# Attention's state as an undecayed dense running sum, and the integer sum of the weights' conversion on VectorE

## The chip, the cores and the metric

The kernel runs on one core of a Trainium2 chip. The metric is the device time of one execution in microseconds (us). The engines are TensorE (PE; PEld is its weight load), VectorE (DVE), ScalarE (ACT), GpSimd (POOL) and SyncE (SP), which here only issues transfers (DMA). Each engine takes its instructions in a fixed order.

## The reference

A retention layer (attention without softmax, with a decay `gamma` of its own for each head) feeds a block with a rational activation, and that feeds a gated block behind an RMS norm. All is in float32; there are 4 sequences of 576 tokens, 8 heads of 64 and a width of 512, so 2304 tokens.

```python
scores = scale * np.matmul(q, k.transpose(0, 1, 3, 2))
Dmat = np.where(rel >= 0, gamma[:, None, None] ** rel[None, :, :], 0.0)   # rel = i - j
x = np.matmul(scores * Dmat, v)                      # [4, 8, 576, 64] -> [2304, 512]
h = x @ w_in                                         # 2048 wide
g = (a0 + a1*h + a2*h**2 + a3*h**3) / (1 + |b0|*|h| + |b1|*h**2 + 1e-6)
x = g @ w_out                                        # 512 wide
xn = x / sqrt(mean(x * x) + 1e-6) * rms_g
out = (silu(xn @ w_gate) * (xn @ w_val)) @ w_out2    # 1536 wide
```

## The kernel before

**Attention.** Each sequence is cut into 5 chunks of 128 tokens (the last has 64), which makes 20 steps. Step `i` works on all 8 heads, as 4 pairs: one head of a pair has its 64 dimensions on partitions 0 to 63, the other on 64 to 127 (`e` is 0 or 1). `att_scores` (L189) multiplies k and q of each pair on PE (L196) and lets DVE multiply the scores with the table `dmk` (L201); `att_out` (L225) adds to one PSUM bank the product of q with the state `S` (L232) and that of the masked scores with v (L238), scales it with `gq` into the one buffer `xe` (L245; the trace calls it `gx`), and sends this to DRAM (L249) or, for the first 384 tokens, splits it for the next block (L211, L212). `att_state` (L253) multiplies k and v (L261), and `att_add` adds this to the state (L275, L277).

The decay sits in four tables: `dmk` is the causal mask times a power of gamma for each key, k is scaled by `gk` on POOL for the state (`prep_k`, L187), the state is scaled by `gs` from one chunk to the next on ACT (`att_decay`, L221), and the output by `gq`. The state of a pair is a 128 x 128 matrix with zeros off the diagonal, in two buffers `SS`, since L232 multiplies both heads of a pair at once; so DVE writes it in two halves of 64 partitions. `dmk` is built at the start by eight products on POOL (L532).

**Weights.** They come as raw 64-bit words. `begin` (L134) turns a tile of 128 x 512 into float32 by hand: two activations on ACT (L141, L142), a shift and a merge on DVE (L143, L147), and the integer sum of high and low part on POOL (L150), after which the raw buffer (one of three) is loaded anew by SP (L129). `finish` (L154) rounds on ACT (L156) and takes the rest on DVE or, for each fourth tile, on POOL (L157). There are 32 tiles for the first block (`wa`) and 36 for the second (`wb`).

**The blocks.** The first block takes 6 blocks of 384 tokens through 16 steps each: `m1_up` (L308 to L310, 12 matmuls), the activation on ACT, DVE and POOL (`m1_el`, L329 to L369), and `m1_down` (L317 to L321, 12 matmuls) three steps later. The first token block runs beside the attention: `hook` places four pieces of a step of the attention between the matmuls, and `wa_step` the conversion of the weights. The norm between the blocks (`be_*`, L387 to L426) and the first weights of the second block lie beside the last steps. The second block is `m2_up` (L440 to L442) and `m2_down` (L457 to L459).

A scheduler with a model of the engines makes the final order of each engine from this program.

## Time and profile before

| what | us |
|---|---|
| median of 3 runs | 1006.39 |
| lowest and highest | 1004.44, 1006.87 |
| the profiled execution | 1000.21 |
| its span in the trace | 998.4 |
| mean granted clock of PE in it | 0.986 |

All rows are of that one execution; its span is shorter than its time by 1.8 us. Where PE is idle, or works at the lower level of its clock, time is lost; an engine that is idle elsewhere costs nothing by that. [...] Windows are counted from the span's start. A row's busy time is the time covered by instructions of that engine.

### The profile page before, as it was taken

How to read it: one execution, taken by the hardware profiler on the slowest of the kernel's cores; microseconds unless marked ns; L12 is line 12 of the kernel's file. 1: busy time of each engine (PE TensorE's matmuls, PEld its weight loads, DVE VectorE, ACT ScalarE, POOL GpSimd, SP SyncE). 2: the span in 40 equal slices, each digit the busy share in tenths (PEclk: the TensorE clock that was granted, in tenths of full speed). 3: DMA queues.
4: the chain of work that ended last, by engine and by line, in shares of the span. 5: the costliest groups of instructions: out<-in, count | busy, mean ns of one | idle time of the engine just before them, and what ended most of it. 6: DMA issues, size and time to landing. Idle time of an engine off the chain costs nothing.

```text
span 998.4 us, 14966 instructions
## 1 busy us (share of the span) xinstructions
PE 970.4 (97%) x5726; PEld 912.7 (91%) x5726; DVE 567.7 (57%) x993; ACT 548.1 (55%) x1076; POOL 390.7 (39%) x358
## 2 busy tenths in 40 slices
PE   8898998999999999999989999999999999999998
PEld 6798887899999999999989989999999999999997
DVE  5989997768667675776697685554212112112111
ACT  4777775776877877878868665554112112111111
POOL 4666674754654746646646423334001001000000
PEclk9899999999999999999999999999999999999999
DMA  9757676300100100001012343433101000000000
GB/s 315 267 174 219 227 239 209 119 5 32 33 1 32 33 33 19 14 32 32 23 56 93 110 136 127 127 125 101 48 1 34 31 1 30 19 1 9 24 1 32
DMA packets 37592, 78.91 MB, mean 79 GB/s; under 512 B 5904, under 2 KB 21392, under 8 KB 37520
## 3 DMA queue, kind: packets, MB, share of 16 engines
q1 hardware_dynamic: 36512, 77.61, 23.8%
q8 instruction: 45, 0.74, 0.3%
q10 hardware_dynamic: 1008, 0.34, 0.1%
q14 instruction: 27, 0.22, 0.1%
HBM read 64.57 MB, written 13.37 MB: 78 GB/s over the span
## 4 chain that ended last, share of the span: by engine, by line
PE 73%; DVE 11%; ACT 4%; issue 4%; DMA 4%; POOL 3%; DVEq 0%; ACTq 0%; SPq 0%; POOLq 0%
PE bank L440 9%; PE bank L442 9%; PE bank L441 9%; PE bank L308 5%; PE bank L458 5%; PE bank L459 5%; PE bank L457 5%; PE bank L310 5%; PE bank L309 5%; PE bank L317 5%; PE bank L318 5%; PE bank L321 4%; DVE w L157 1%; DMA raw<-in_w_out_dram 1%; DMA x_d<-gx 1%
## 5 line engine op out<-in xcount | busy, mean ns | idle before, releaser
L440 PE MATMUL bank<-x,w 128*128 128x384 f32 x528 | 177.2, 336 | 1.9 <-DVE sg L446 1.9
L442 PE MATMUL bank<-x,w 128*128 128x384 f32 x528 | 177.2, 336 | 0.0
L441 PE MATMUL bank<-x,w 128*128 128x384 f32 x528 | 177.0, 335 | 0.0
L446 DVE TENSOR_TENSOR sg<-sg,bank 128x384 f32<-128x384 f32 x72 | 39.8, 553 | 213.8 <-PE bank L442 213.7
L150 POOL TENSOR_TENSOR ft<-ft,raw 128x512 int32<-128x512 int32 x68 | 94.8, 1396 | 119.9 <-DVE ft L147 78.4
L308 PE MATMUL bank<-x,w 128*128 128x384 f32 x384 | 132.4, 346 | 5.1 <-DVE u L350 4.8
L348 POOL TENSOR_TENSOR q<-q,ah 128x384 f32<-128x384 f32 x96 | 101.4, 1057 | 85.2 <-ACT q L344 81.6
L309 PE MATMUL bank<-x,w 128*128 128x384 f32 x384 | 131.1, 341 | 1.3 <-DVE x L212 1.3
L310 PE MATMUL bank<-x,w 128*128 128x384 f32 x384 | 131.1, 341 | 0.0
L369 POOL TENSOR_TENSOR g<-u,g 128x384 fp32r<-128x384 f32 x96 | 100.8, 1051 | 69.5 <-issue 34.4
L317 PE MATMUL bank<-g,w 128*128 128x384 f32 x384 | 124.7, 341 | 3.2 <-ACT g L367 3.2
L318 PE MATMUL bank<-g,w 128*128 128x384 f32 x384 | 123.5, 338 | 0.6 <-POOL w L157 0.6
L445 ACT ACTIVATE sg<-bank 128x384 f32<-128x384 f32 x72 | 35.3, 490 | 152.6 <-PE bank L442 152.4
L212 POOL TENSOR_TENSOR x<-xr,x 128x384 fp32r<-128x384 f32 x44 | 46.5, 1069 | 158.0 <-ACT x L211 157.8
L440 PEld LDWEIGHTS bank<-x,w 128*128 128x128 f32 x528 | 99.1, 188 | 5.6 <-DVE sg L446 2.2
L441 PEld LDWEIGHTS bank<-x,w 128*128 128x128 f32 x528 | 99.1, 188 | 3.0 <-POOL x L212 0.3
L442 PEld LDWEIGHTS bank<-x,w 128*128 128x128 f32 x528 | 99.1, 188 | 0.1
L448 ACT ACTIVATE y<-sg 128x384 fp32r<-128x384 f32 x72 | 37.6, 523 | 100.7 <-DVE sg L446 99.9
L349 DVE TENSOR_TENSOR u<-u,bank 128x384 f32<-128x384 f32 x96 | 52.9, 551 | 60.3 <-ACT u L345 59.5
L321 PE MATMUL bank<-g,w 128*128 128x384 f32 x384 | 85.3, 336 | 0.0
L308 PEld LDWEIGHTS bank<-x,w 128*128 128x128 f32 x384 | 73.7, 192 | 8.3 <-DVE u L350 6.6
L317 PEld LDWEIGHTS bank<-g,w 128*128 128x128 f32 x384 | 71.4, 189 | 5.3 <-ACT g L367 4.0
(92 smaller groups left out, 2042.6 us busy)
## 6 DMA issues: line engine op xcount, KB each, us to landing
raw<-in_w_out_dram SPq DMA_DIRECT2D x28, 512.0 KB, 3.7
xb<-in_qkT_dram SPq DMA_DIRECT2D x19, 512.0 KB, 4.9
kv<-in_kv_dram SPq DMA_DIRECT2D x16, 512.0 KB, 5.3
raw<-in_w_in_dram SPq DMA_DIRECT2D x16, 512.0 KB, 4.1
raw<-in_w_gate_dram SPq DMA_DIRECT2D x12, 512.0 KB, 3.4
raw<-in_w_val_dram SPq DMA_DIRECT2D x12, 512.0 KB, 3.4
xn_d<-x SPq DMA_DIRECT2D x6, 768.0 KB, 3.8
xr<-xn_d SPq DMA_DIRECT2D x24, 192.0 KB, 2.5
```

Of the source, the lines that this page charges most:

```text
L150: pool.tensor_tensor(out=ft, in0=ft, in1=lo, op=ALU.add)
L308: pe.matmul(out=h, lhsT=w[:, 0, ks], rhs=x[:, 0, k], start=(k == 0), stop=False)
L309: pe.matmul(out=h, lhsT=w[:, 0, ks], rhs=x[:, 1, k], start=False, stop=False)
L310: pe.matmul(out=h, lhsT=w[:, 1, ks], rhs=x[:, 0, k], start=False, stop=(k == KD - 1))
L317: pe.matmul(out=acc[m], lhsT=w[:, 0, ms], rhs=g[:, 0], start=(j == 0), stop=False)
L318: pe.matmul(out=acc[m], lhsT=w[:, 1, ms], rhs=g[:, 0], start=False, stop=False)
L321: pe.matmul(out=acc[m], lhsT=w[:, 0, ms], rhs=g[:, 1], start=False, stop=(j == J1 - 1))
L348: pool.tensor_tensor(out=q, in0=q, in1=ah, op=ALU.mult)
L369: eng.tensor_tensor(out=g[:, 1], in0=p, in1=g[:, 0].bitcast(F32), op=ALU.subtract)
L440: pe.matmul(out=t, lhsT=w[:, 0, ks], rhs=x[:, 0, k], start=(k == 0), stop=False)
L441: pe.matmul(out=t, lhsT=w[:, 0, ks], rhs=x[:, 1, k], start=False, stop=False)
L442: pe.matmul(out=t, lhsT=w[:, 1, ks], rhs=x[:, 0, k], start=False, stop=(k == KD - 1))
```

## The change

The decay leaves the state, the scores and k. Each v is scaled by gamma to minus its position (counted from the middle of the sequence), the output by gamma to its position, and the scores only get the causal mask of zeros and ones. So the state is a plain running sum of k times v: `att_decay` and its 48 activations go, `S` is one buffer without the zeros, and DVE updates it in one instruction on 128 partitions. The product of q with the state becomes 8 matmuls on 64 x 64 quarters of the array instead of 4 on the whole. POOL scales v (`prep_v`) where it scaled k, also in the last chunk, and its eight products for the table fall away; `gq` has a table for each of the five chunks, four of them loaded by SP in the first steps. In the last chunk the keys of the second head lie on partitions 64 to 127, and k isn't loaded. `xe` has a buffer of its own; it is still one.

The integer sum of each weight tile moves from POOL to DVE, all 68 of them. [...]

```diff
-    gk = at_p.tile([128, NH, 1], F32, name="gk")
-    gs = at_p.tile([128, NP, 1], F32, name="gs")
-    gi = at_p.tile([128, NH, 1], F32, name="gi")
+    gv = at_p.tile([128, NC, NH, 1], F32, name="gv")
+    msk = at_p.tile([128, 1, CH], F32, name="msk")
...
-    dmk = borrow("dmk").rearrange("p (e n c) -> p e n c", e=2, n=NP)
-    gx = borrow("gx").rearrange("p (a n c) -> p a n c", a=2, n=NP)
-    gq, xe = gx[:, 0], gx[:, 1]
-    SS = [at_p.tile([128, NP, 2, HD], F32, name=f"S{i}") for i in range(2)]
+    gq = []
+    for i in range(2):
+        t = borrow(f"gq{i}").rearrange("p (a n c) -> p a n c", a=2, n=NP)
+        gq += [t[:, 0], t[:, 1]]
+    gq.append(at_p.tile([128, NP, SEQ - (NC - 1) * CH], F32, name="gq4"))
+    xe = at_p.tile([128, NP, CH], F32, name="xe")
+    S = at_p.tile([128, NP, HD], F32, name="S")
...
-            pool.tensor_tensor(out=ft, in0=ft, in1=lo, op=ALU.add)
+            dve.tensor_tensor(out=ft, in0=ft, in1=lo, op=ALU.add)
...
+    def keys(i, e):
+        n = size(steps[i][1])
+        return n, slice(0, n) if n == CH else slice(n * e, n * e + n)
...
     def load_kv(i, dq=sp):
         if i < len(steps):
-            n = size(steps[i][1])
-            dq.dma_start(out=kv_b[i % 3][0:n], in_=kv[steps[i]][0:n])
-
-    def prep_k(i, eng):
-        if i < len(steps) and steps[i][1] < NC - 1:
-            k = kv_b[i % 3][:, 0]
-            eng.tensor_tensor(out=k, in0=k, in1=gk.to_broadcast([128, NH, HD]), op=ALU.mult)
+            c = steps[i][1]
+            if c < NC - 1:
+                dq.dma_start(out=kv_b[i % 3], in_=kv[steps[i]])
+            else:
+                n = size(c)
+                for e in range(2):
+                    dq.dma_start(
+                        out=kv_b[i % 3][n * e:n * e + n, 1], in_=kv[steps[i]][0:n, 1]
+                    )
+
+    def prep_v(i, eng):
+        if i < len(steps):
+            v = kv_b[i % 3][:, 1]
+            eng.tensor_tensor(
+                out=v, in0=v, in1=gv[:, steps[i][1]].to_broadcast([128, NH, HD]), op=ALU.mult
+            )
+
+    def load_gq(c):
+        if c < NC:
+            n = size(c)
+            sp.dma_start(out=gq[c], in_=t_gq[c, :, :, 0:n])
...
-                out=sc[0:n, p, 0:n], lhsT=qk[r, 1, p, 0:n], rhs=qk[r, 0, p, 0:n],
+                out=sc[ks, p, 0:n], lhsT=qk[r, 1, p, 0:n], rhs=qk[r, 0, p, 0:n],
...
-            out=rets[i, e][0:n, :, 0:n], in0=sc[0:n, :, 0:n], in1=dmk[0:n, e, :, 0:n], op=ALU.mult
+            out=rets[i, e][ks, :, 0:n], in0=sc[ks, :, 0:n],
+            in1=msk[ks, :, ks].to_broadcast([n, NP, n]), op=ALU.mult,
...
-    def att_decay(i):
-        c = steps[i][1]
-        if 0 < c < NC - 1:
-            for p in range(NP):
-                act.activation(
-                    out=SS[(c + 1) % 2][:, p], in_=SS[c % 2][:, p], func=ACTF.Copy, scale=gs[:, p]
-                )
...
             for p in range(NP):
-                pe.matmul(
-                    out=o[:, p, 0:n], lhsT=SS[c % 2][:, p].rearrange("p a d -> p (a d)"),
-                    rhs=q[:, p, 0:n], start=(p == 0), stop=False, skip_group_check=True,
-                )
+                for e in range(2):
+                    r = slice(64 * e, 64 * e + 64)
+                    pe.matmul(
+                        out=o[r, p, 0:n], lhsT=S[r, p], rhs=q[r, p, 0:n],
+                        start=(p == 0), stop=False, skip_group_check=True,
+                    )
         for p in range(NP):
             for e in range(2):
                 pe.matmul(
-                    out=o[64 * e:64 * e + 64, p, 0:n], lhsT=v[0:n, 2 * p + e],
-                    rhs=rets[i, e][0:n, p, 0:n], start=(c == 0 and p == 0), stop=(p == NP - 1),
+                    out=o[64 * e:64 * e + 64, p, 0:n], lhsT=v[keys(i, e)[1], 2 * p + e],
+                    rhs=rets[i, e][keys(i, e)[1], p, 0:n], start=(c == 0 and p == 0), stop=(p == NP - 1),
                     skip_group_check=True,
                 )
         t0 = b * SEQ + c * CH
         xo = xe[:, :, 0:n]
-        dve.tensor_tensor(out=xo, in0=o[:, :, 0:n], in1=gq[:, :, 0:n], op=ALU.mult)
+        dve.tensor_tensor(out=xo, in0=o[:, :, 0:n], in1=gq[c][:, :, 0:n], op=ALU.mult)
...
         if not pend:
             return
         c, ds = pend.pop()
-        new = SS[(c + 1) % 2]
-        for e in range(2):
-            r = slice(64 * e, 64 * e + 64)
-            if c == 0:
-                dve.tensor_copy(out=new[r, :, e], in_=ds[r])
-            else:
-                dve.tensor_tensor(out=new[r, :, e], in0=new[r, :, e], in1=ds[r], op=ALU.add)
+        if c == 0:
+            dve.tensor_copy(out=S, in_=ds)
+        else:
+            dve.tensor_tensor(out=S, in0=S, in1=ds, op=ALU.add)
...
     def att_jobs(kind, first, end):
         for i in range(first, end):
             att_add()
-            att_decay(i)
             load_kv(i + 2)
+            load_gq(i + 1)
             att_scores(i + 1, 0, kind)
             yield
...
-            prep_k(i + 1, pool)
+            prep_v(i + 1, pool)
...
-    for i in range(2):
-        dve.memset(SS[i], 0.0)
+    dve.memset(xe, 0.0)
     dve.memset(ones, 1.0)
-    warm = SS[0].rearrange("p n a d -> p (n a d)")
+    warm = xe.rearrange("p n c -> p (n c)")
...
-    act.dma_start(out=gq, in_=t_gq)
+    act.dma_start(out=msk, in_=t_dm)
     for a in range(2):
         sp.dma_start(out=qk_b[0][:, a], in_=qkT[0, 0, :, a])
-    act.dma_start(out=dmk[:, 0, 0], in_=t_dm)
-    act.dma_start(out=gi, in_=t_gi)
-    dmk8 = dmk.rearrange("p e n c -> p (e n) c")
-    for h in range(NH - 1, -1, -1):
-        pool.tensor_tensor(
-            out=dmk8[:, h], in0=dmk8[:, 0], in1=gi[:, h].to_broadcast([128, CH]), op=ALU.mult
-        )
+    act.dma_start(out=gq[0], in_=t_gq[0])
     act.activation(out=qb, in_=ones[:, 0:2], func=ACTF.Abs)
     load_kv(0, sp)
-    act.dma_start(out=gk, in_=t_gk)
-    act.dma_start(out=gs, in_=t_gs)
+    act.dma_start(out=gv, in_=t_gv)
...
-    t_gq = (HD ** -0.5) * g_pair[:, :, None] ** pos
-    t_gk = (gam[None, :] ** (CH - pos)[:, None])[:, :, None]
-    t_gs = (g_pair ** CH)[:, :, None]
+    rel = (np.arange(NC * CH) - SEQ // 2).reshape(NC, CH)
+    t_gq = (HD ** -0.5) * g_pair[None, :, :, None] ** rel[:, None, None, :]
+    rel[-1, CH // 2:] = rel[-1, :CH // 2]
+    t_gv = gam ** (-1.0 * rel.T[:, :, None])
     t_dm = pos[None, :] >= pos[:, None]
-    t_gi = (gam[None, :] ** (-1.0 * pos[:, None])).reshape(CH, NP, 2).transpose(0, 2, 1)
...
```

The order moves with it. On DVE, in the first steps of the attention, where `ret` are masked scores, `S` the state, `ft` and `w` the weights in conversion, before:

```order
L201 TENSOR_TENSOR ret<-bank_103,dmk 128x512
L143 TENSOR_SCALAR ft<-ft 128x512
L245 TENSOR_TENSOR gx<-bank_105,gx 128x512
L147 SCALAR_TENSOR_TENSOR ft<-raw,ft 128x512
L201 TENSOR_TENSOR ret<-bank_102,dmk 128x512
L143 TENSOR_SCALAR ft<-ft 128x512
L212 TENSOR_TENSOR x<-gx,x 128x4x128
L147 SCALAR_TENSOR_TENSOR ft<-raw,ft 128x512
L201 TENSOR_TENSOR ret<-bank_103,dmk 128x512
L157 TENSOR_TENSOR w<-ft,w 128x512
L277 TENSOR_TENSOR S_115<-S_115,bank_104 64x4x64 x2
```

and now (L219 was L201, L258 was L245, L231 was L212, L287 was L277):

```order
L258 TENSOR_TENSOR xe<-bank_105,gq_112 128x512
L147 SCALAR_TENSOR_TENSOR ft<-raw,ft 128x512
L143 TENSOR_SCALAR ft<-ft 128x512
L219 TENSOR_TENSOR ret<-bank_102,msk 128x512
L150 ISA ft<-raw,ft 128x1024
L231 TENSOR_TENSOR x<-xe,x 128x4x128
L147 SCALAR_TENSOR_TENSOR ft<-raw,ft 128x512
L219 TENSOR_TENSOR ret<-bank_103,msk 128x512
L157 TENSOR_TENSOR w<-ft,w 128x512
L287 TENSOR_TENSOR S<-S,bank_104 128x256
L150 ISA ft<-raw,ft 128x1024
```

The sums stand in DVE's row two or three instructions behind the merge (L147), and a state's update is one instruction.

On SP at the end of the attention, where `x_d<-` stores a step's output and `xr<-x_d` loads the next token blocks, before:

```order
L249 DMA x_d<-gx 512x1x128
L182 DMA kv_111<-in_kv_dram 64x1024
L249 DMA x_d<-gx 512x1x128 x2
L479 DMA xr<-x_d 128x384 x2
L249 DMA x_d<-gx 512x1x64
L479 DMA xr<-x_d 128x384 x2
```

and now (L262 was L249, L489 was L479):

```order
L262 DMA x_d<-xe 512x1x128
L191 DMA kv_110<-in_kv_dram 64x512 x2
L262 DMA x_d<-xe 512x1x128
L489 DMA xr<-x_d 128x384 x2
L262 DMA x_d<-xe 512x1x128
L489 DMA xr<-x_d 128x384 x2
L262 DMA x_d<-xe 512x1x64
```

Two pairs of loads stand ahead of the last store now, where one stood before. On PE, between the last two steps' products with v, there are 23 matmuls of the first block before and 50 now.

On DVE beside the norm of the fifth token block, some 500 us into the trace (`ss` is the norm's sum, `x_4840<-` its product with the tokens, `q`, `u` and the banks belong to the activation of the last block), before:

```order
L329 SCALAR_TENSOR_TENSOR q<-q,bank_105 128x384
L415 TENSOR_TENSOR ss<-ss,y 128x384
L329 SCALAR_TENSOR_TENSOR q<-q,bank_104 128x384
L330 SCALAR_TENSOR_TENSOR bank_105<-q,bank_105 128x384
L416 SCALAR_TENSOR_TENSOR ss<-ss,y 128x384
L349 TENSOR_TENSOR u<-u,bank_103 128x384
L330 SCALAR_TENSOR_TENSOR bank_104<-q,bank_104 128x384
L332 SCALAR_TENSOR_TENSOR u<-u,cf,bank_105 128x384
L421 SCALAR_TENSOR_TENSOR x_4840<-x_4840,rg,ss 128x384 x4
L350 SCALAR_TENSOR_TENSOR u<-u,cf,bank_103 128x384
```

and now (each of these lines is ten further down):

```order
L339 SCALAR_TENSOR_TENSOR q<-q,bank_105 128x384
L150 ISA ft<-raw,ft 128x1024
L425 TENSOR_TENSOR ss<-ss,y 128x384
L339 SCALAR_TENSOR_TENSOR q<-q,bank_104 128x384
L340 SCALAR_TENSOR_TENSOR bank_105<-q,bank_105 128x384
L359 TENSOR_TENSOR u<-u,bank_103 128x384
L426 SCALAR_TENSOR_TENSOR ss<-ss,y 128x384
L340 SCALAR_TENSOR_TENSOR bank_104<-q,bank_104 128x384
L342 SCALAR_TENSOR_TENSOR u<-u,cf,bank_105 128x384
L360 SCALAR_TENSOR_TENSOR u<-u,cf,bank_103 128x384
L431 SCALAR_TENSOR_TENSOR x_4841<-x_4841,rg,ss 128x384 x4
```

The last reader of bank_103 (L350, now L360) has moved from behind the four products of the norm to ahead of them.

## Rows read from the trace of the kernel before

**Rows 1.** The page, part 1: busy us (share of the span) x instructions.

```profile
PE 970.4 (97%) x5726; PEld 912.7 (91%) x5726; DVE 567.7 (57%) x993; ACT 548.1 (55%) x1076; POOL 390.7 (39%) x358
```

**Rows 2.** Windows: us, busy us of each engine (x instructions), PE's clock, DMA share, GB/s.

```profile
11.00:32.00 21.00, 17.63 (x194) 14.83 (x192) 20.64 (x32) 13.53 (x30) 9.46 (x9) 1.00 0.93 317
11.00:169.00 158.00, 148.11 (x1236) 130.38 (x1234) 144.16 (x240) 112.54 (x227) 99.68 (x80) 0.95 0.73 238
169.00:205.00 36.00, 31.71 (x221) 29.98 (x222) 24.82 (x43) 26.14 (x56) 27.32 (x25) 0.91 0.30 92
205.00:495.00 290.00, 288.91 (x1653) 286.39 (x1653) 206.66 (x383) 226.88 (x456) 165.72 (x166) 1.00 0.08 24
495.00:520.00 25.00, 21.09 (x111) 20.50 (x110) 22.56 (x40) 19.13 (x38) 11.23 (x11) 0.93 0.15 53
```

**Rows 3.** Waits of DVE, 11 to 169 us (us, times, longest), and POOL's timeline.

```profile
DVE ret L201 <- POOL dmk L532: 9.1, 1, 9.1
DVE u L349 <- ACT u L345: 2.4, 4, 1.5
DVE q L329 <- ACT bank L361: 1.9, 3, 0.9
...
11.11 1.04 POOL L187 TENSOR_TENSOR kv<-kv,gk 128x512 f32<-128x512 f32 x1
```

**Rows 4.** Groups of DVE by line and form, 11 to 169 us: busy us, mean ns.

```profile
L147 DVE SCALAR_TENSOR_TENSOR ft<-raw,ft 128x512 int32<-128x512 int32 x29 | 25.6, 883 | 0.3
L157 DVE TENSOR_TENSOR w<-ft,w 128x512 fp32r<-128x512 f32 x21 | 21.7, 1038 | 0.1
L201 DVE TENSOR_TENSOR ret<-bank,dmk 128x512 f32<-128x512 f32 x31 | 21.2, 683 | 9.6 <-POOL dmk L532 9.1 <-PE bank L196 0.4
L143 DVE TENSOR_SCALAR ft<-ft 128x512 int32<-128x512 int32 x29 | 16.7, 574 | 0.0
...
L277 DVE TENSOR_TENSOR S<-S,bank 64x256 f32<-64x256 f32 x20 | 8.3, 415 | 0.1
...
L275 DVE COPY S<-bank 64x256 f32<-64x256 f32 x8 | 3.3, 418 | 1.4 <-PE bank L261 1.3
```

**Rows 5.** Lines L147, L157 and L143, 0 to 205 us: shortest/median/longest ns.

```profile
L147 DVE SCALAR_TENSOR_TENSOR ft<-raw,ft x32: 676/694/1662, 15.1 to 184.7; 128x512 int32<-128x512 int32 x32
...
L157 DVE TENSOR_TENSOR w<-ft,w x24: 678/983/1551, 20.1 to 187.8; 128x512 fp32r<-128x512 f32 x24
...
L143 DVE TENSOR_SCALAR ft<-ft x32: 405/420/1402, 14.2 to 183.2; 128x512 int32<-128x512 int32 x32
```

**Rows 6.** Groups of POOL, 11 to 169 us: busy us, mean ns | idle before.

```profile
L150 POOL TENSOR_TENSOR ft<-ft,raw 128x512 int32<-128x512 int32 x29 | 39.5, 1367 | 26.6 <-issue 8.8 <-DVE ft L147 6.3 <-ACT ft L141 3.5
```

**Rows 7.** Timeline of PE (start, us), and a piece of the chain.

```profile
13.02 1.09 PE L238 MATMUL bank<-ret,kv 128*64 128x128 f32 x16
16.97 1.16 PE L232 MATMUL bank<-xb,S 128*128 128x128 f32 x8
...
126.35 0.17 PE bank L309
```

**Rows 8.** Timeline of SP and DVE at the end of the attention.

```profile
162.46 0.53 SPq L249 DMA_DIRECT2D x_d<-gx  x1
...
169.05 0.69 DVE L245 TENSOR_TENSOR gx<-bank,gx 128x512 f32<-128x512 f32 x1 [2.34 <-DMA x_d<-gx]
```

**Rows 9.** Waits from 500 to 512 us, and DVE's timeline there.

```profile
PE bank L308 <- DVE u L350: 3.9, 1, 3.9
...
503.09 0.54 DVE L329 SCALAR_TENSOR_TENSOR q<-q,bank 128x384 f32<-128x384 f32 x1
503.55 1.20 DVE L415 TENSOR_TENSOR ss<-ss,y 128x384 f32<-128x384 f32 x1
...
507.93 2.93 DVE L421 SCALAR_TENSOR_TENSOR x<-x,rg,ss 128x384 f32<-128x384 f32 x4
510.78 0.60 DVE L350 SCALAR_TENSOR_TENSOR u<-u,cf,bank 128x384 f32<-128x384 f32 x1
```

More of the change, by code (lines that the diff above doesn't have):

```diff
@@ L52, in retention_moe_kernel @@
     t_gq: bass.AP,
-    t_gk: bass.AP,
-    t_gs: bass.AP,
+    t_gv: bass.AP,
     t_dm: bass.AP,
-    t_gi: bass.AP,
     out: bass.AP,
@@ L191, in att_scores @@
             return
-        n = size(steps[i][1])
+        n, ks = keys(i, e)
         qk, r = qk_b[i % 3], slice(64 * e, 64 * e + 64)
@@ L548, in retention_moe_kernel @@
     att_scores(0, 1, "h")
-    prep_k(0, pool)
+    prep_v(0, pool)
     for s, _ in enumerate(att_jobs("h", 0, P0)):
@@ L752 @@
         ("t_gq", t_gq.astype(np.float32)),
-        ("t_gk", t_gk.astype(np.float32)),
-        ("t_gs", t_gs.astype(np.float32)),
-        ("t_dm", t_dm.astype(np.float32)),
-        ("t_gi", t_gi.reshape(CH, NH, 1).astype(np.float32)),
+        ("t_gv", t_gv[..., None].astype(np.float32)),
+        ("t_dm", t_dm[:, None].astype(np.float32)),
     ]
```

## The prediction

> **What bounds the kernel now.** Read the busy shares first: TensorE (PE) is busy for 97% of the span [rows 1], so only the stretches where it isn't can give or take time. The windows view finds them [rows 2]: from 205 to 495 us PE is busy 288.91 of 290 us, and nothing that VectorE (DVE), ScalarE (ACT) or GpSimd (POOL) saves there reaches the end. PE idles in three places: 11 to 169 us (the attention beside the first token block), 169 to 205 (its end), and 495 to 520. In the first, DVE is busy 144.16 of 158 us, 91%, and PE 148.11, but at a mean clock of 0.95; PE's busy time there holds waits between pipelined matmuls, DVE's does not. I take DVE as the engine that sets the pace there, with ACT (112.5) and POOL (99.7) in second place. This matters because the change takes work from POOL and ACT and gives work to DVE.
>
> **The change part by part, 11 to 169 us.** This is DVE's account; 29 of the 68 weight tiles are converted in this stretch [rows 4].
> - Added: 29 integer sums on DVE. No row shows this instruction. Below, it can't be cheaper than L147, which goes through the same 512 words from two SBUF tensors: 0.676 us at the least [rows 5]. Above, its stream is 1024 half words; L201 takes 0.683 us for 512 elements and L329 0.54 for 384 [rows 4, 9], so 1024 one by one would take 0.683 + 4 x 0.143 = 1.25 us. I take the lower end, since the row that it is nearest to in words moved is L147's. Consecutive DVE instructions overlap a little: the L329 at 503.09 takes 0.54 and the next starts 0.46 later [rows 9]; less 0.08, one sum occupies 0.60: 29 x 0.60 = +17.4.
> [...]
> - Removed: the state was updated in two halves of 64 partitions, now in one instruction. A half takes 0.415 us [rows 4], the whole has as many elements in a lane and costs the same: 14 fewer x 0.35 occupied = -4.9.
> - Contention. DVE's instructions with two SBUF operands, and L143, are slower while POOL works: L147 0.883 us in the mean against 0.676 at the least, L157 1.038 against 0.678, L143 0.574 against 0.405 [rows 4, 5]; together 29 x 0.207 + 21 x 0.360 + 29 x 0.169 = 18.5 us, with POOL busy for 63% of the stretch [rows 2]. POOL loses 39.5 us of sums (L150) [rows 6] and gains three more products of 1.04 us [rows 3] (v of the last chunk is scaled too): 99.7 - 39.5 - 0.4 + 3.1 = 62.9, about 39%. The exposed work grows from 29 x (0.676 + 0.405) + 21 x 0.678 = 45.6 to 65.3 us. Scaled by both: 18.5 x 65.3 / 45.6 x 39 / 63 = 16.4, so -2.1.
> - Sum: DVE's work goes from 144.2 to 154.6 us, +10.4.
> - The start: DVE's first product waited 9.1 us for POOL's last mask product, which ended when POOL went on at 11.11 [rows 3] and is gone now (the mask now comes whole by DMA). The next gates are the first scores and the coefficients' DMA, which stands ahead of the product in the new order; I take -1.0 (0 to -1.2).
> How much of +10.4 reaches the end hangs on DVE's idle 14 us. If DVE fills 96% (it was 20.64 of 21 us in the first part, 98% [rows 2]; 91% over all), the stretch starting at 10.2 ends at 10.2 + 154.6 / 0.96 = 171.2 instead of 169: **+2.2**. At 91% it ends at 180 (+11), at 100% at 164.8 (-4.2).
>
> ACT loses its 48 small scalings of the state. DVE waits for ACT only 4.3 us in the stretch [rows 3], so I count nothing of it by itself; what it shortens is part of how well DVE fills. Four more loads of the output's decay (3 x 256 KB + 128 KB = 0.92 MB) go onto SP's queue ahead of the fourth chunk's q, k and v. DMA is 93% busy from 11 to 32 us [rows 2], so those land later by 0.92 MB at 317 GB/s = 2.9 us; the third chunk's work, which comes first, lies over that: nothing (0 to +2).
>
> On PE the product of q with the state goes from 4 full-array matmuls to 8 on diagonal quarters of the array. Before, 4 of them take 1.16 us (8 records); v's product, 8 matmuls of 64 columns, takes 1.09 for 16 records, so two halves of the array run together [rows 7]. If the quarters do so too, 1.16 becomes 1.09: 16 steps, -1 us of PE time, nothing at the end. If they don't, each step costs 2.2.
>
> [...]
>
> **169 to 205 us.** At the end of the attention each of its 20 steps waits for the single output buffer: the 17th step's output leaves at 162.46, DVE waits 2.34 us for that store and writes the 18th's at 169.05 [rows 8], 6.6 us a step. Under this the old order has 23 MoE matmuls between the last two steps' outputs, at 0.17 us [rows 7] 3.9 us; the new has 50, 8.5 us, and that covers the loop. It also puts the second token block's loads (xr) one step earlier on SP's queue. PE idles 4.3 us in this window, with a clock of 0.91 [rows 2]. I take the uncovered part, 6.6 - 3.9 = **-2.7** (0 to -5).
>
> **495 to 520 us.** PE waits 3.9 us for L350 [rows 9], which frees a bank. L350 stands behind the four L421 (2.93 us from 507.93) in DVE's queue, and ends at 511.38. In the new order it stands ahead of them. Counting on from the L329 at 503.09 in steps of what each occupies: 503.56, sum 0.60, L415 0.47 (it took 1.20 beside POOL's sum, which is gone), L329, L330, L349 3 x 0.47, L416 0.9, L330 0.47, L332 0.53, L350 0.60: 508.5. That is **-2.9**. [...]
>
> From 520 to 700 us the other 36 sums stand where PE, saturated or nearly so, hides them.
>
> **The sum.** +2.2 - 2.7 - 2.9 = -3.4 us. The profiled execution took 1000.21 us (span 998.4), 6.2 less than the median of 1006.39; I take the difference over to the median: 1003.0.
>
> **The rivals.**
> - A, slower: DVE doesn't fill better. It is idle because the work passes in turn through PE, ACT and DVE, so it stays at 91%, and the stretch ends at 180. For it: 2.4 + 1.9 us of DVE's idle time are waits for ACT in this very loop [rows 3]. Against: 98% in the first part. +11 - 2.7 - 2.9 = +5.4: 1012. Below a filling of about 94% (10.2 + 154.6 / 0.94 = 174.7, +5.7) it outweighs the two gains and the kernel is slower than before.
> - B, slower: the half words pass one by one. 29 x 0.57 x 1.2 for contention = 20 us more on DVE; at 96% that is +21 - 3.4: 1024.
> - C: the quarters don't run together: 12 full steps x 1.1 + 4 half ones x 0.55 = 15 us more on PE, of which its 9.9 idle us in the stretch [rows 2] and the 2.2 of its lengthening hide most: +3, or up to +8 where PE's idle pieces lie elsewhere than the steps; 1008. [...]
> - D, no change: the new order's gains at 169 to 205 and 507 aren't there, because engines reach those places at other times; +2.2 remains: 1008.6 with nothing of them, 1006 with half.
> - E, faster: the loop through POOL decided more than DVE's load. L150 waited and kept the raw buffer from its next load (8.8 us of idle time before it with no cause shown, [rows 6]); the sum now follows two or three instructions behind L147 on the same queue. DVE fills 100%: -4.2 - 5.6 = -9.8: 997.
>
> **How the numbers follow.** Chances: forecast 0.37, A 0.18, B 0.06, C 0.11, D 0.16, E 0.12. About 0.3% (3 us) is what a measurement of this kernel can tell from no change, and the forecast at -3.4 lies on that edge: of its 0.37, 0.22 is faster and 0.15 the same. With E 0.12, faster 0.34; same is 0.15 + D's 0.12 + C's 0.05 = 0.32; slower is A, B, the rest of C and D: 0.34. Range for 8 in 10: 996 (just under E) to 1014 (A and C, with 2 us for the start's loads); it leaves out B. The forecast's own range is 998 to 1007.
>
> **What the profile after would show.** DVE's sum (L150) at 0.6 to 0.7 us where POOL is idle, its mean near 0.8; 1.2 or more would be B. DVE's busy share to the 18th step's output 95 to 97% for the forecast, 91% for A, with that output near 171 us against 169. The state's product (16 records) in about 1.1 us; 2.2 would be C. L147 and L157 nearer to their least. No wait of PE for the u of L350's successor over 1.5 us near 507, and from 169 to 205 less PE idle than 4.3 us. I am wrong if DVE's work in the stretch grew by much less or more than 10 us, or if the new order puts a new stall of PE after 205 us, which I have not found.

## The result: faster by 1.0%, three times the forecast

The changed kernel takes 994.29 us in the median of 8 runs (988.04 to 999.02), the kernel before beside it 1006.63: ratio 0.990, 95% interval 0.987 to 0.993, 10 us less. Forecast were 1003.0, 3.4 less, with a range down to 996: 994.29 lies 1.7 below that end, and the ratio applied to the 1006.39 that the forecast started from gives 996.1, just on it. The sign holds; the size doesn't. Over the later runs of this study and all runs of the changed kernel, the kernel before has a median of 1003.4 (94 runs), the changed one of 994.0 (18): 9.4 us. I use these two below.

The runs of one kernel differ by up to 14 us (before) and 11 us (changed), so one profile of each would mislead. Two executions of each were profiled: before at 1000.21 and 1008.09 us, after at 997.74 and 987.93. To compare them I cut each at one instruction of TensorE that all share: the sum over partitions for the norm of the fifth block (L404, in the changed kernel L414). What lies ahead of it is the **head** (it holds the attention), what lies behind, to the end of the span, the **tail**. The timeline's rows (start, us of all, matmul records) of before, before again, after, after again:

```profile
498.39 0.81 PE L404 MATMUL bank<-ss,ones 128*128 128x384 f32 x2
...
505.01 0.81 PE L404 MATMUL bank<-ss,ones 128*128 128x384 f32 x2
...
498.49 0.81 PE L414 MATMUL bank<-ss,ones 128*128 128x384 f32 x2
...
488.73 0.81 PE L414 MATMUL bank<-ss,ones 128*128 128x384 f32 x2
```

With spans of 998.4, 1006.3, 995.8 and 986.0 the tails are 500.0 and 501.3 before, 497.3 and 497.3 after: the tail hardly varies and is 3.4 us shorter. The heads vary by 7 to 10 us between executions of one kernel. Medians less the tail and the 1.8 or 1.9 us outside the span put the head at 500.9 before and 494.8 after: 6.1 us of the gain lie there. The second profile of each kernel is called "again" below.

The page and the windows of after (997.74 us), answering to [rows 1, 2]; columns as there:

```profile
PE 971.1 (98%) x5854; PEld 909.9 (91%) x5854; DVE 588.3 (59%) x1044; ACT 530.5 (53%) x1026; POOL 296.8 (30%) x286
...
11.00:32.00 21.00, 18.48 (x170) 15.28 (x166) 16.95 (x28) 9.62 (x16) 3.73 (x3) 0.75 0.95 339
169.00:205.00 36.00, 35.60 (x297) 32.48 (x298) 24.70 (x44) 21.74 (x44) 19.81 (x20) 0.91 0.38 113
495.00:520.00 25.00, 22.75 (x127) 21.53 (x126) 22.25 (x41) 19.50 (x39) 10.10 (x10) 1.00 0.16 52
```

TensorE's idle time from 169 to 205 us went from 4.3 us to 0.4, and from 495 to 520 us it is busy 22.75 us at a clock of 1.00 (of full speed) instead of 21.09 at 0.93. The first window shows where the heads begin to scatter. Here it is again in the other execution of after and the other one of before:

```profile
11.00:32.00 21.00, 18.66 (x209) 15.60 (x208) 19.62 (x33) 10.51 (x18) 4.59 (x4) 1.00 1.00 365
...
11.00:32.00 21.00, 20.60 (x168) 17.90 (x164) 16.72 (x28) 11.75 (x27) 7.53 (x6) 0.67 0.72 248
```

Both kernels have executions in which the clock stays at 1.00 in this window and executions in which it falls for most of it (0.75 and 0.67 in the mean; in after it is at 0.50 from 22 to 38 us), with the same order of instructions. With the fall, TensorE does 170 records instead of 209 (before: 168 instead of 194).

VectorE's groups of after, 11 to 169 us, answering to [rows 4], and the sum's shortest, median and longest ns up to 205 us, answering to [rows 5]:

```profile
L147 DVE SCALAR_TENSOR_TENSOR ft<-raw,ft 128x512 int32<-128x512 int32 x29 | 24.7, 861 | 0.2
L150 DVE CUSTOM_DVE_ANT_0 ft<-raw,ft 128x1024 uint16<-128x1024 uint16 x29 | 24.3, 839 | 0.2
L157 DVE TENSOR_TENSOR w<-ft,w 128x512 fp32r<-128x512 f32 x21 | 16.2, 770 | 0.4 <-ACT w L156 0.3
L143 DVE TENSOR_SCALAR ft<-ft 128x512 int32<-128x512 int32 x29 | 15.4, 537 | 2.8 <-ACT ft L141 2.7
L287 DVE TENSOR_TENSOR S<-S,bank 128x256 f32<-128x256 f32 x9 | 3.7, 411 | 0.0
...
L150 DVE CUSTOM_DVE_ANT_0 ft<-raw,ft x32: 670/683/1659, 15.8 to 189.9; 128x1024 uint16<-128x1024 uint16 x32
```

The sum of a tile's 512 words is one instruction over 1024 half words (uint16), which takes 0.670 us at the least and 0.839 in the mean. The state's update is one instruction of 0.41 us instead of two.

### The profile page after: what moved, and what is told of

The parts are those of the page before. It is cut to its first block, busy times and chain, and to the rows that moved or that the text cites. A ratio compares the mean times of both kernels' runs of the same rounds, so it can differ in the third digit from the quotient of the medians.

```text
span 995.8 us, 15066 instructions
## 1 busy us (share of the span) xinstructions
PE 971.1 (98%) x5854; PEld 909.9 (91%) x5854; DVE 588.3 (59%) x1044; ACT 530.5 (53%) x1026; POOL 296.8 (30%) x286
## 5 line engine op out<-in xcount | busy, mean ns | idle before, releaser
L231 POOL TENSOR_TENSOR x<-xr,x 128x384 fp32r<-128x384 f32 x44 | 46.2, 1063 | 284.1 <-ACT x L230 284.1
L327 PE MATMUL bank<-g,w 128*128 128x384 f32 x384 | 128.0, 340 | 2.3 <-ACT g L377 2.2
L328 PE MATMUL bank<-g,w 128*128 128x384 f32 x384 | 126.5, 335 | 0.0
L450 PEld LDWEIGHTS bank<-x,w 128*128 128x128 f32 x528 | 99.1, 188 | 5.7 <-DVE sg L456 0.9
L451 PEld LDWEIGHTS bank<-x,w 128*128 128x128 f32 x528 | 99.1, 188 | 3.0 <-POOL x L231 0.3
L452 PEld LDWEIGHTS bank<-x,w 128*128 128x128 f32 x528 | 99.1, 188 | 0.4
L331 PE MATMUL bank<-g,w 128*128 128x384 f32 x384 | 86.6, 336 | 0.0
L318 PEld LDWEIGHTS bank<-x,w 128*128 128x128 f32 x384 | 73.7, 192 | 10.1 <-DVE u L342 5.0
L320 PEld LDWEIGHTS bank<-x,w 128*128 128x128 f32 x384 | 73.7, 192 | 0.5 <-issue 0.3
```

The lines of the kernel that those rows point to most:

```text
L318: pe.matmul(out=h, lhsT=w[:, 0, ks], rhs=x[:, 0, k], start=(k == 0), stop=False)
L320: pe.matmul(out=h, lhsT=w[:, 1, ks], rhs=x[:, 0, k], start=False, stop=(k == KD - 1))
L327: pe.matmul(out=acc[m], lhsT=w[:, 0, ms], rhs=g[:, 0], start=(j == 0), stop=False)
L328: pe.matmul(out=acc[m], lhsT=w[:, 1, ms], rhs=g[:, 0], start=False, stop=False)
L331: pe.matmul(out=acc[m], lhsT=w[:, 0, ms], rhs=g[:, 1], start=False, stop=(j == J1 - 1))
L450: pe.matmul(out=t, lhsT=w[:, 0, ks], rhs=x[:, 0, k], start=(k == 0), stop=False)
```

## The experiments

**The two parts apart.** Theory "order": the gain sits where the order of instructions changed. Rival "loop" (E of the prediction): it comes from taking GpSimd out of the conversion's chain. The sum alone is one line in the kernel before; the attention alone is the changed kernel with that line undone.

```diff
-            pool.tensor_tensor(out=ft, in0=ft, in1=lo, op=ALU.add)
+            dve.tensor_tensor(out=ft, in0=ft, in1=lo, op=ALU.add)
```

> The kernel before with one line changed: the integer sum on VectorE; the attention stays as it was. Theory order: the gain of the whole change sits in two places where the order of instructions changed, 169 to 205 us and 495 to 520 us, and neither is new here (27 rather than 50 records between the last two outputs, and L350 still stands behind the four norm products), while VectorE carries about 8 us more net work up to 169 us: 1008 to 1014 us, and the wait of 3.9 us for L350 near 507 us is still there. Rival loop (rival E of the prediction): taking GpSimd out of the conversion's chain is what gains, so the sum alone gives most of it: 997 to 1001 us.

> The changed kernel with the integer sum back on GpSimd: the change of the attention alone. Theory order: VectorE has about 5 us less work up to 169 us, the start is 2 us earlier, and 169 to 205 us has the new order (-2.8), while L360 still stands behind the norm products near 507 us: 999 to 1003 us. Rival loop: GpSimd keeps its sums and gets three more products, so only the start and the end of the attention gain: 1002 to 1006 us, and the sum alone (e1) has the rest.

The sum alone: 1015.03 us, ratio 1.011 (1.008 to 1.015), slower. The attention alone: 996.54 us, ratio 0.992 (0.989 to 0.994), better than both theories gave. Their cuts, and what lies behind the cut in the kernel before and with the sum alone (columns as in [rows 2]):

```profile
511.48 0.81 PE L404 MATMUL bank<-ss,ones 128*128 128x384 f32 x2
...
490.82 0.81 PE L414 MATMUL bank<-ss,ones 128*128 128x384 f32 x2
...
498.39:998.39 500.00, 489.05 (x2573) 458.01 (x2572) 188.29 (x318) 177.70 (x332) 91.87 (x74) 1.00 0.17 55
...
511.48:1018.59 507.11, 494.95 (x2597) 464.49 (x2596) 206.10 (x358) 177.84 (x338) 47.32 (x42) 0.99 0.17 54
```

With the sum alone, TensorE has 24 records of the blocks more behind the cut than the kernel before and as many fewer ahead of it; at 0.173 us from one to the next in the timeline they are 4.2 us of work. The other kernels have 2573 there, as before. So in the table 4.2 us are taken from the tail of the sum alone and added to the stretch ahead of the cut. A second cut, the end of the 18th step's output on VectorE, parts the head in two. It ends at 169.74 us [rows 8] before, and:

```profile
176.40 0.69 DVE L245 TENSOR_TENSOR gx<-bank,gx 128x512 f32<-128x512 f32 x1 [1.10 <-PE bank L238]
...
178.17 0.68 DVE L258 TENSOR_TENSOR xe<-bank,gq 128x512 f32<-128x512 f32 x1
...
169.08 0.68 DVE L258 TENSOR_TENSOR xe<-bank,gq 128x512 f32<-128x512 f32 x1
...
188.92 0.69 DVE L245 TENSOR_TENSOR gx<-bank,gx 128x512 f32<-128x512 f32 x1 [1.43 <-PE bank L238]
...
166.83 0.69 DVE L258 TENSOR_TENSOR xe<-bank,gq 128x512 f32<-128x512 f32 x1
```

These are before again, after, after again, the sum alone and the attention alone. The last two columns of the table come from the profiles (for before and both the mean of two), the first is what the medians leave:

| kernel | to the 18th output | against before | from there to the cut | against before | tail | against before |
|---|---|---|---|---|---|---|
| before | 172.6 | | 328.3 | | 500.7 | |
| sum alone | 183.8 | +11.2 | 326.0 | -2.3 | 502.9 | +2.2 |
| attention alone | 166.9 | -5.7 | 323.3 | -5.0 | 504.5 | +3.8 |
| both | 175.5 | +2.9 | 319.3 | -9.0 | 497.3 | -3.4 |

The first column carries the scatter of the medians, some 2 to 3 us. The other two are steadier. Four profiles with the old attention and the sum on GpSimd (the two of before, and two of the experiments below) have 327.3 to 329.0 from the 18th output to the cut and a tail of 500.0 to 501.5. Six with the new attention and all sums on VectorE have 319.0 to 321.2 and 497.2 to 497.5. The parts have one profile each.

So up to the 18th output VectorE's sums cost and the new attention gains, and the loop through GpSimd gains nothing there: +11.2 - 5.7 = +5.5, measured +2.9, apart by no more than the scatter. From there to the cut the whole change gains more than its parts (-7.3 together). In the tail each part alone is longer and both together are shorter. The waits of the attention alone, 490 to 510 us, and of the sum alone, 515 to 565 us (us, times, longest):

```profile
PE bank L318 <- DVE u L360: 3.9, 1, 3.9
...
PE bank L440 <- ACT sg L445: 4.4, 1, 4.4
```

With the attention alone L360 still stands behind the four norm products, the very wait of [rows 9]; with the sum alone there is another, of 4.4 us, in the second block's first steps. Of these only the whole change has L360 ahead, which ends at 508.17 us:

```profile
507.57 0.60 DVE L360 SCALAR_TENSOR_TENSOR u<-u,cf,bank 128x384 f32<-128x384 f32 x1
508.10 2.95 DVE L431 SCALAR_TENSOR_TENSOR x<-x,rg,ss 128x384 f32<-128x384 f32 x4
```

**Both kernels once more**, to see what the scatter is.

> The kernel before once more, unchanged, to see why its median (1006.6 us) lies 6.4 us over the execution that was profiled (1000.2). Theory clock: the executions differ by how long TensorE stands at its lower clock in the first 205 us; each run's mean granted clock falls with its time, about 0.010 of clock for 7 us, and a profile near 1006 shows some 6 us more lost to the lower level than the first profile's 13.5, with the same stalls. Rival: an additional stall of TensorE (a late transfer) explains it; then the clock is the same in long and short runs and the profile has a wait of 4 us or more that the first doesn't have.

> The changed kernel once more, unchanged, 988 to 999 us so far. Theory clock: the runs near 988 have a mean clock of 0.994 to 0.996, those near 998 have 0.982 to 0.984; a profile of a short run lacks the 17 us at the lower clock from 21.6 us on that the first profile shows. Rival: the difference is a stall or a transfer, and the clock follows it.

Medians 1005.61 and 993.72 us. The times lie on lines over each run's mean granted clock: -0.64 us for 0.001 in 94 runs of before (0.971 to 0.991), -0.78 in 18 of after (0.982 to 0.996). No execution has a stall that its twin lacks by 4 us, so "clock" describes the scatter. (Beside the 1005.61 of its 10 runs here, 25 more runs of the kernel before had a median of 1002.46: medians of one kernel can differ by 3 us.) The means of the clock are 0.9805 before and 0.9886 after, those of the time 1003.8 and 993.3; with one slope for all kernels of this study (0.65), they stand at 1000.8 and 995.6 us at a clock of 0.985. So of these 10.5 us 5.2 are there at an equal clock, and the other 5.3 (0.0081 x 0.65 for 0.001) go with a higher clock in the changed kernel's runs. Whether the clock brings these 5.3 or only follows from shorter idle pieces of TensorE is the next question.

**Filling TensorE's early idle time**, in the changed kernel and in the kernel before:

```diff
     for s, _ in enumerate(att_jobs("h", 0, P0)):
+        qw = qk_b[(s // 4 + 1) % 3]
+        for i in range(2):
+            pe.matmul(out=banks[i][:, 0:128], lhsT=qw[:, 1, i], rhs=qw[:, 0, i], start=True, stop=True)
```

> The changed kernel with 24 more matmuls (q by k of the step at hand, 128 columns over the whole array, into two banks that hold nothing yet; nothing reads them) among those of the first three attention steps, where TensorE has idle pieces of up to 2 us. So far the changed kernel's runs lie on a line of -0.69 us for 0.001 of mean clock (995.8 us at 0.985), and the first 60 us hold most of the half-clock time. Theory clock: with the idle pieces filled the clock doesn't fall there; the runs' mean clock is 0.992 or more in nearly all runs, and the median 988 to 991 us. Rival: the clock isn't what costs time, it only reads lower where the engine idles or the fall comes from elsewhere: the fillers' own 5.1 us (24 x 0.213) are half hidden, 994 to 998 us, and the clock's scatter stays at 0.982 to 0.996.

> The same 24 filler matmuls in the kernel before. Theory clock: its runs have a mean clock of 0.980 and lie at 1003.8 us, 1000.5 at 0.985, on a line of -0.63 us for 0.001; filled, the early fall of the clock (13.7 us at the lower level from 12.3 us in the execution of 1008 us) goes, the clock is 0.988 or more and the median 996 to 999 us: then most of what the change gained over the line (6 of 10.5 us) was this clock. Rival: 1002 to 1006 us with the clock as before.

In both profiles the clock is at 1.00 where the fillers stand. In the changed kernel 6 of their records take 0.94 us and 14 take 1.83, so 0.22 us for each filler (two records), where the expectation had 0.213. Two windows of the filled changed kernel, where they stand and later:

```profile
11.00:32.00 21.00, 19.29 (x223) 17.06 (x222) 18.41 (x32) 11.66 (x20) 5.39 (x5) 1.00 0.92 329
157.00:174.00 17.00, 14.07 (x105) 12.25 (x104) 6.20 (x11) 1.77 (x4) 4.36 (x5) 0.54 0.60 182
```

But the times are 1002.71 and 1020.79 us, 9 and 17 us worse than without, and the clock still scatters (0.977 to 0.991, and 0.970 to 0.980). In this profile TensorE idles 2.9 us of the 17 from 157 us on, and the clock is at 0.54 there. That the fillers put the idle time there, by delaying matmuls that others wait for, is argued and not shown. Both theories fail: the rival's scatter came true, its price was too low. A higher clock at one place can't be bought this way, and the early fall is not by itself what decides.

**The start alone**: the kernel before with the eight mask products on VectorE.

```diff
-        pool.tensor_tensor(
+        dve.tensor_tensor(
             out=dmk8[:, h], in0=dmk8[:, 0], in1=gi[:, h].to_broadcast([128, CH]), op=ALU.mult
```

> The kernel before with its eight mask products at the start (L532) on VectorE, which is idle there, rather than on GpSimd: the start of the changed kernel alone, no other part of it. VectorE's first score product, at 11.19 us before, comes about 2 us earlier, and TensorE's idle piece at 9.3 to 11.8 us goes. In the executions of 1008 us (before) and 1019 us (sum alone) the clock falls at 12.3 and 12.8 us, right behind that piece, and stays down 13.7 us. Theory start: this is why the kernel before has the lower mean clock; it rises from 0.980 to 0.985 or more, and the median from 1003.8 us comes to 997 to 1000. Rival: the later falls of the clock and the idle pieces up to 205 us decide; only the 1 to 2 us of the earlier start are won, or they are hidden: 1002 to 1004 us with a clock of 0.980.

VectorE's first score product starts at 9.75 us instead of 11.19. Result: 1001.12 us against 1003.32 beside it, ratio 0.998 (0.995 to 1.000), with a mean clock of 0.9841 instead of 0.9808. The time lies between the theory's 1000 and the rival's 1002, and the interval's upper end is no gain at all. The start is at most a part of the attention's gain, not its core.

**The third chunk's load first**, ahead of two weight tiles on SP's queue:

```diff
-            load_kv(i + 2)
+            if i:
+                load_kv(i + 2)
...
     wa.load()
+    load_kv(2, sp)
     wa.load()
     wa.load()
```

> The changed kernel with the load of the third chunk's k and v ahead of two of the first three weight tiles on SP's queue, not behind them: TensorE's wait of 1.5 to 2.1 us for that v near 18 us, behind which the clock falls for 17.1 us in the execution of 998 us, should shrink by 1.5 us or more; the weight tiles come some 1.3 us later. Theory: this idle piece decides between the clocks of 0.982 and 0.996: the runs gather at 0.990 or more, median 987 to 990 us. Rival: the idle time moves to the weights or the clock falls elsewhere instead: 992 to 996 us with the same scatter.

It is 1008.05 us, 14 worse. The load did come earlier, and TensorE's wait moved to where the late weights put VectorE's next instructions:

```profile
19.19 0.33 PE L274 MATMUL bank<-kv 128*64 128x64 f32 x2
21.15 3.06 PE L214 MATMUL bank<-xb 64*128 64x128 f32 x16 [1.63 <-DVE ft L143]
```

The idle time moved, as the rival said, but the price (and a mean clock of 0.9762) lies far beyond it. The scheduler's order changed behind this place too, so the 14 us aren't the load's alone; I haven't taken them apart.

**The added loads.** ScalarE makes the output's decay of each chunk from the one before, in place of the four loads of 0.92 MB:

```diff
-            sp.dma_start(out=gq[c], in_=t_gq[c, :, :, 0:n])
+            for p in range(NP):
+                act.activation(out=gq[c][:, p], in_=gq[c - 1][:, p, 0:n], func=ACTF.Copy, scale=gs[:, p])
```

> The changed kernel without the four added loads (0.92 MB) of the output's decay: ScalarE makes each from the one before with four small scalings (16 instructions in all), from a table of 2 KB. The prediction put the loads at nothing (0 to +2). Theory DMA: TensorE waits 1.6 to 2.1 us near 20 us for the third chunk's v, whose load shares the queue with these; it comes about 0.6 to 1.3 us earlier, the wait shrinks and the clock falls less often there: 989 to 992 us. Rival nothing: the queue makes it up, and ScalarE's 16 instructions cost as much: 993 to 996 us.

995.78 us (991.47 to 998.72), ratio 0.991 (0.988 to 0.994): as the changed kernel. So the loads cost no more than the 16 scalings in their place; either by itself isn't measured.

**VectorE as the pace-setter**, with more work and with less:

```diff
+            dve.tensor_scalar(
+                out=ft, in0=ft, scalar1=0x7FFFFFFF, scalar2=0x7FFFFFFF, op0=ALU.bitwise_and, op1=ALU.bitwise_and,
+            )
```

> The changed kernel with one more VectorE instruction for every weight tile (a mask that changes nothing, in place, as long as L143: 0.405 us at the least, 0.54 in the mean): 30 of them up to the 18th step's output, 12 to 16 us. Theory pace (the prediction's account): VectorE sets the pace of the attention's stretch at a filling of 90 to 94%, so the time grows by that: 1005 to 1011 us. Rival slack: with the new attention TensorE's losses there come from the clock and from loops through other engines, and VectorE's idle 10 us take half or more of it: 995 to 1002 us.

```diff
-            wa.step(dve if wa.n1 % 4 else pool)
+            wa.step(dve if wa.n1 % 2 else pool)
```

> The changed kernel with every second, not every fourth, of the second token-block weights' last subtraction (L157) on GpSimd while the attention runs: some 7 of 21 leave VectorE (0.70 us occupied each, -5 us) and cost GpSimd 1.27 us each; GpSimd is busy 39% there. Theory pace: VectorE (92% busy up to the 18th step's output) sets the end of this stretch, which becomes 3 to 4 us shorter: 989 to 991 us. Rival chain: the stretch is set by the passing of work between ScalarE, VectorE and TensorE, and a slower subtraction lengthens it: 993 to 997 us.

More work: 1004.88 us (12 runs, 1002.39 to 1006.53), 10.9 over the changed kernel, of which 3.4 lie in the tail (its cut is at 502.71 us, its span 1003.4) and some 7 in the head. The added instructions there, 11 to 205 us, took 21.3 us:

```profile
L147 DVE TENSOR_SCALAR ft<-ft 128x512 int32<-128x512 int32 x32 | 21.3, 664 | 0.1
```

So a third of what was put on VectorE there reached the end of the head. Less work: 992.96 us (6 runs, 990.14 to 1003.67), ratio 0.990 (0.985 to 0.995), as the changed kernel, though six L157 fewer (15 against 21) ran on VectorE up to 169 us. "Pace" holds in sign for more work and falls in size: 1004.88 is just under its 1005, but the work put on was 21.3 us and not 12 to 16. Less work shows nothing.

**The sum split by stage.** If head and tail are separate accounts, the best is the attention alone's head with the changed kernel's tail: GpSimd sums for the first layer's weights, VectorE for the second's.

```diff
-            dve.tensor_tensor(out=ft, in0=ft, in1=lo, op=ALU.add)
+            self.add.tensor_tensor(out=ft, in0=ft, in1=lo, op=ALU.add)   # pool in wa, dve in wb
```

> The changed kernel with the integer sum on GpSimd for the 32 weight tiles of the first token-block layer (converted beside the attention), on VectorE for the 36 of the second (converted from 430 to 580 us): the attention's stretch is that of the attention alone (e2), the order behind it that of the changed kernel, with L361 (the changed kernel's L360) ahead of the four norm products. Theory places: the gains and losses sit in separate stretches and add up. The attention alone loses 4.1 us at 499 us, 2.6 at 529 and 2.0 at 576 to waits and two falls of the clock, the changed kernel 2.5, 1.4 and 0.8 without a fall, some 7 us less: 996.2 - 7 = 988 to 991 us, 3 to 5 below the changed kernel. Rival: VectorE's sums beside the attention cost nothing in the changed kernel (its first 205 us are as short as with GpSimd's), so this one stands where the changed kernel does, 992 to 996 us.

988.92 us (985.54 to 991.01), ratio 0.986 (0.982 to 0.989): the fastest of all, 5 us below the changed kernel. Its cut and, 490 to 510 us, its longest wait of TensorE:

```profile
491.00 0.81 PE L415 MATMUL bank<-ss,ones 128*128 128x384 f32 x2
...
PE bank L328 <- ACT g L378: 1.6, 1, 1.6
```

The head (491.0) is that of the attention alone (490.8), the tail (988.3 - 491.0 = 497.3) that of the changed kernel. Here the accounts add up.

## Why the prediction was right in sign and too small

- **What the sum costs by itself**: right. Forecast 0.6 to 0.7 us where GpSimd is idle and near 0.8 in the mean; 0.670 and 0.839. Rival B (1.25 us) is out. So 1024 half words take what L147 needs for 512 words, 0.676 us at the least; the forecast's choice of the lower end was an estimate from that row.
- **Contention**: right in sum. Over their least, L147, L157, L143 and the sum lose 29 x 0.185 + 21 x 0.092 + 29 x 0.132 + 29 x 0.169 = 16.0 us; forecast 16.4. That the loss goes with GpSimd's work shows in before, 0 to 205 us: L147 takes 0.68 us in the 13 instructions beside which GpSimd is idle, and 1.17 in the mean (up to 1.66) in the 12 with GpSimd busy for over half of their time; L201, which reads a bank, takes 0.69 and 0.68.
- **VectorE's account up to the 18th output**: right in size, by two errors that cancel. Forecast +2.2, measured by the medians +2.9. Of this the forecast gave the sum +8.3 and the attention -4.9 / 0.96 - 1.0 = -6.1; the table has 175.5 - 166.9 = +8.6 for the sum on top of the new attention, and -5.7 for the attention. But I let VectorE's work grow by 10.4 us and its filling rise from 91 to 96%. The windows up to the 18th step's output (columns as in [rows 2]), of before, before again, after, after again:

```profile
10.20:169.74 159.54, 148.61 (x1240) 130.68 (x1238) 144.86 (x242) 112.98 (x227) 100.70 (x82) 0.95 0.73 237
...
10.20:177.09 166.89, 158.30 (x1235) 139.60 (x1236) 146.24 (x241) 113.59 (x227) 100.73 (x82) 0.88 0.69 227
...
8.87:178.85 169.98, 156.75 (x1357) 134.79 (x1357) 152.76 (x260) 102.24 (x185) 66.11 (x56) 0.90 0.69 232
...
8.95:169.76 160.81, 145.47 (x1363) 125.55 (x1362) 149.94 (x259) 102.15 (x184) 68.47 (x56) 0.98 0.73 245
```

VectorE is busy 144.86 and 146.24 us before, 152.76 and 149.94 after, 4 to 8 more with one more weight tile converted, and fills 91 and 88% before, 90 and 93% after. The filling is nearer to rival A's than to mine, the work grew by less than I said, and that the two cancel is luck. TensorE's 1357 and 1363 records instead of 1240 and 1235 are hardly more work: 112 are the eight small products more in each of 14 steps; of the blocks it has done 331 and 334 instead of 324, 1.2 to 1.7 us at 0.173 us each. That TensorE's busy time there isn't work alone shows in the records of one form: L308's take 0.370 us in the mean from 11 to 169 us before, at a clock of 0.95, and 0.337 from 205 to 495, at 1.00.
- **The start**: forecast -1.0 (0 to -1.2), measured by e11 about -2, with an interval that reaches to no gain.
- **169 to 205 us**: the term that was mis-sized, and the step that failed. Forecast -2.7 (0 to -5); from the 18th output to the cut it is -9.0, and this difference of 6.3 us is what the whole forecast lacks (6.0). The 36 us behind the 18th output, in the order as above:

```profile
169.74:205.74 36.00, 32.45 (x225) 30.72 (x226) 24.87 (x43) 25.69 (x54) 27.10 (x25) 0.91 0.30 92
...
177.09:213.09 36.00, 31.87 (x233) 30.10 (x232) 25.55 (x45) 26.33 (x56) 26.73 (x25) 0.95 0.31 92
...
178.85:214.85 36.00, 36.00 (x285) 34.22 (x284) 27.26 (x51) 29.55 (x61) 24.09 (x24) 1.00 0.31 92
...
169.76:205.76 36.00, 36.00 (x286) 34.45 (x285) 27.96 (x52) 30.36 (x63) 24.46 (x25) 1.00 0.32 92
```

TensorE's idle time there goes from 3.6 and 4.1 us to nothing. The clock goes from 0.91 and 0.95 to 1.00, which is 3.2 and 1.8 of 36 us; the forecast had put nothing for the clock here. With the 1.2 to 1.7 us of the blocks' work that is now done ahead, these are 7 to 8.5 of the 9.0. The reason that I gave, the loop through the single output buffer, is the smaller part. It held TensorE up for 1.04 us before, up to 169.88, so hardly behind the 18th output, and not at all before again, where no output of the last four waits for a store. TensorE's long wait in this window is for ScalarE's g in both, and ScalarE had waited for the second token block's tokens 12 to 13 us ahead of it:

```profile
188.17 0.53 ACT L211 ACTIVATE x<-xr 128x384 fp32r<-128x384 f32 x1 [1.87 <-DMA xr<-x_d]
200.53 0.44 PE L317 MATMUL bank<-g,w 128*128 128x384 f32 x1 [2.65 <-ACT g L367]
...
194.22 0.53 ACT L211 ACTIVATE x<-xr 128x384 fp32r<-128x384 f32 x1 [1.87 <-DMA xr<-x_d]
207.27 0.69 PE L317 MATMUL bank<-g,w 128*128 128x384 f32 x1 [3.35 <-ACT g L367]
```

Between the two ScalarE has one gap over 0.2 us in the second pair (0.74, for such tokens again) and none in the first, so its late start there reaches g. In both profiles of after TensorE doesn't wait there, and ScalarE waits for those tokens 0.7 us at the longest. The new order has both the 50 matmuls and the earlier loads, which the prediction named without a price; which of them does it, no run shows, so the cause of this gain stays open to that extent.
- **495 to 520 us**: right to the instruction. L360 was to end at 508.5 us, 10.1 behind the cut, and ends at 508.17, 9.7 behind it; -2.9 was forecast, and the tail is 3.4 us shorter, with the clock's fall gone (1.00 for 0.93 from 495 to 520 us). Neither part alone has this order.
- **The quarters of the array**: right, rival C is out. A timeline of after has the state's product at both clocks, beside v's product, whose halves share rows:

```profile
14.66 1.09 PE L245 MATMUL bank<-xb,S 64*64 64x128 f32 x16
...
25.72 1.97 PE L251 MATMUL bank<-ret,kv 128*64 128x128 f32 x14
...
29.62 1.97 PE L245 MATMUL bank<-xb,S 64*64 64x128 f32 x16
```

The product's 16 records take 1.09 us at a clock of 1.00, as forecast for quarters that run together and half of rival C's 2.2, and 1.97 at 0.50 (22 to 38 us), where 14 records of v's product take 1.97 too. The quarters of a pair write different partitions of one bank.
- **The loads** at nothing: not contradicted by e8, which put 16 scalings in their place and took as long.
- **Rival E** named a time (9.8 us less) that came true, for a reason that didn't: with GpSimd out of the chain and nothing else changed, the kernel is slower.

So 3.4 us of the 9.4 are the tail, forecast as 2.9, and 9.0 the last steps of the attention and what follows to the cut, forecast as 2.7; up to the 18th output 2.9 are lost, forecast as 2.2. How the attention's 5.7 up to the 18th output are shared by the start, the shorter state update, ScalarE's 48 scalings and the granted clock, I couldn't part. Why the new attention's executions keep the higher clock more often (0.9888 in the mean of the attention alone, 0.9805 before) stays open: with the early idle time filled it was at 1.00 where the fillers stood, and the runs' mean was no higher.

## What to carry to other kernels

Cut the profile where one engine is saturated, count that as much work lies ahead of the cut in every kernel, and keep an account for each piece: here the parts of a change nearly added up in one piece and did the opposite in another, where the order of a queue decided, and the best kernel took each part only where it paid. A forecast can be right in one piece for the wrong reason and miss in the next; the total shows neither. An engine at 90% isn't yet the one that sets the end: put some more work on it and see how much arrives (here 7 of 21.3 us). Where runs of one kernel scatter, look at the granted clock of each before comparing two profiles, and compare at an equal clock.

## What was unexpected

- The kernel before runs at a mean granted clock of 0.971 to 0.991 and takes 997 to 1011 us along with it, some 0.64 us for 0.001; the fall can come or not come at the same place in the same order of instructions (0.67 and 1.00 from 11 to 32 us before, 0.75 and 1.00 after).
- With more matmuls in TensorE's idle pieces the clock was at 1.00 there in both profiles, and the kernels were 9 and 17 us slower.
- At the end of the attention TensorE waited longest for an activation (2.65 and 3.35 us), not for the output buffer that the steps share, and the largest gain is in this stretch.
- An integer sum over 1024 half words takes VectorE no longer (0.670 us) than an operation over 512 words from two tensors (0.676).
